# Block-sparse attention and a hard-swish MLP: values and their neighbour rows loaded by casting DMAs, head pairs p and p+4

## The chip, the cores and the metric

The kernel runs on one core of a Trainium2 chip. The metric is device time in microseconds (us); the profile's span goes from the first to the last instruction of one profiled execution.

## The reference

```python
B, H, S, D = 4, 8, 768, 64;  block, window = 32, 16;  scale = 1 / sqrt(D)
k_sum = max of k over each block of 32 rows       # 24 blocks a head
v_sum = mean of v over each block
scores_l = where(|i - j| < window, scale * q @ k.T, -1e9)
scores_s = scale * q @ k_sum.T + log(block)
a = softmax over [scores_l, scores_s]
x = a @ [v, v_sum]                                # (B, H, S, D) -> (B*S, H*D)
h = x @ w_in                                      # 512 -> 2048
out = (h * clip(h + 3, 0, 6) / 6) @ w_out         # 2048 -> 512
```

q, k, v, w_in, w_out and the output are f32. `kernel(q, k, v, moe_w_in, moe_w_out)` gives 3072 x 512.

## The kernel before, in words

**Tiles.** A query block is 64 rows, so a head has NQ = 12 of them. A query block sees at most 128 keys: its own 64 keys (partitions 0 to 63), the 24 block summaries (R_SUM = 64 to 87, with zeros to 95), the first 16 keys of the next block (R_NEXT = 96 to 111) and the last 16 of the block before (R_PREV = 112 to 127). `kx` holds these 128 key columns of each block, `qx` the transposed queries, `at` the exponentials, and `va[0]`, `va[1]` (even and odd batches) the 128 value rows in the same order, bf16. Two heads form a pair; a pair's rows in `va` are value of head j = 0, 64 columns between, value of j = 1, so that one 128 wide weight covers a head's values and the columns between, which hold zeros or (DEN_IN_VALUES, batches 2 and 3) the weights that give the softmax's denominator. Pairs are heads 2p and 2p+1.

**Attention of a batch b and pair p.** `Tk` (L484) transposes staged k on PE, copies it to `kx` on ACT (L502), reduces the block maxima on DVE (L513), spreads them over the blocks (L518), and copies the 16-column edges (L523, L525). `Tq` (L537) does the same for q (L550, L560). `Sc` (L573) makes the scores of half the query blocks (L591), their exp on ACT (L595), and the mask: batch 0 adds a mask on PE first (L586, `MASK_ON_PE`), the others multiply by 0 or 1 on DVE (L598). `AV` (L609) multiplies by the values (L625) and, in batches 0 and 1, by ones for the denominator (L630), takes 1/den as exp(-ln) on ACT (`lg`, L638 to L642), and writes `x` on DVE (L651 to L654). The value and denominator PSUM tiles have one buffer each.

**Feed-forward.** A tile t is half a batch, 384 rows of x. `F1(t, ft)` is four matmuls of 384 columns (`hp`, L678), a relu on ACT (`r`, L683) and a product on DVE (`g`, L686); `F2(t, j)` is three matmuls of 512 columns (L707); the copy out of PSUM is ACT's (L712), the store SP's (L714). F1 of a tile needs x of all four pairs.

**How v gets into `va` before.** Batches 0 and 1: `load_vf` (L252) reads v as f32 with 128 rows on the partitions; `cast_v` (L265) casts it into `va` on ACT, DVE and POOL; `edges_v` (L278, L279) copies the neighbours' rows from `va` to `va` with SP's DMAs, after the casts. Batch 0's block sums are matmuls with an indicator (`sum_v`, L736), copied by DVE (L740) and by POOL (`put_sums`, L751). Batches 2 and 3: `load_v` (L288) reads one head into `va` with a casting DMA, `edges_v` copies neighbours after all heads. Batches 1 to 3 get their block sums from `load_vrows` (L295), which reads 32 rows of a block into one partition, a tree of adds on POOL (`vsum`, L307) and SP's DMAs that write the sums into `va` (L311). `weights_between` and `zero_va1` (L757 to L774) fill the constant parts on POOL.

**What sets the order.** `Plan` (L33) collects every operation with an engine, a cost, a place in a list of slots, what it reads and writes and which buffers it takes; `order` (L63) simulates the engines with these costs and writes the instructions out in that order, each engine's in a fixed sequence. On the chip an engine waits at an instruction until its data are there, so nothing overtakes. All loads are issued by POOL, on one software queue, with eight completion semaphores in turn: a load's issue waits until the load eight before it has landed. The neighbour copies, sums and stores are issued by SP. The places are given by `first(p)` (L784) for batch 0, and by slots: F1 of tiles 0 and 1 in slots 0 to 31, F2 of tile 1 in 32 to 51, the loads of batch 1 at slot 14, its attention from slot 20, and so on (L809 to L874):

```python
    for b, s in ((2, 50), (3, 82)):
        at_slot(s, loads_kq, b, 0)
        at_slot(s + 8, loads_kq, b, 2)
        at_slot(s + 8.1, loads_v, b)
    for b in range(1, B):
        attention(b, 48 + 32 * (b - 1))
```

`first_loads_1` (L820) orders batch 1's loads, sums, casts and neighbour copies.

Of the kernel before, what the change touches and what calls it, by code (L numbers as in the profile page):

```python
# [25 lines left out]
NLONG = 4  # L26
NFILL = 100
MASK_ON_PE = (0,)
# [4 lines left out]
class Plan:  # L33
# [4 lines left out]
    BUFS = {"h": 2, "o": 2, "s": 2, "num": 1, "den": 1, "kq": 4, "g": 3, "x": 3, "vr": 2, "r": 3, "ot": 3, "lg": 2, "red": 2}  # L38
    CROSS = 0.18
    DMA_FIRST, DMA_SP = 1.4, 2.0  # L40
    WARM, SPARE = 7.0, 24.0
# [21 lines left out]
    def order(self):  # L63
# [3 lines left out]
        queue = 0.0  # L67
        given = {}

        turn = {q: [k for o in self.ops for pool, k in o["takes"] if pool == q] for q in ("x", "g", "vr")}  # L70
# [6 lines left out]
        while ready:  # L77
            cand = {}
            for i in ready:
# [7 lines left out]
                if any(pool in turn and turn[pool][len(given.get(pool, ()))] != key for pool, key in o["takes"]):  # L87
                    continue
                for n_th, (pool, key) in enumerate(o["takes"]):
                    old = given.get(pool, []) + [k for q, k in o["takes"][:n_th] if q == pool]  # L90
                    if len(old) >= self.BUFS[pool]:
                        for u in self.users.get(old[-self.BUFS[pool]], ()):
                            if end[u] is None:
                                ok = False
                                break
                            t = max(t, end[u] + self.CROSS)
                    if not ok:
                        break
                if ok:
                    cand.setdefault(o["eng"], []).append((t, o["place"], i))  # L100
# [17 lines left out]
            if o["dma"]:  # L118
                if o["eng"] == "POOL":
                    queue = max(queue, t + cost + self.DMA_FIRST) + o["dma"]  # L120
                    end[i] = queue
                else:
                    end[i] = t + cost + self.DMA_SP + o["dma"]
            for pool, key in o["takes"]:
                given.setdefault(pool, []).append(key)
# [24 lines left out]
def kernel(  # L150
# [43 lines left out]
    va = [const.tile([128, NP, NQ, 3, D], BF16, tag=f"va{i}", name=f"va{i}") for i in range(2)]  # L194
# [5 lines left out]
    def stage(which, b, p, half=None):  # L200

        if b == 0 and which == "k":
            return f"k{p // 2}", 2 * (p % 2), 4, RUN
        if b == 0:
            return f"q{half}", 2 * p, 8, RUN // 2
        return f"{which}{b}{p // 2}", 2 * (p % 2), 4, RUN
# [3 lines left out]
    def staged(which, b, p, half=None):  # L210
        name, i, n, r = stage(which, b, p, half)
        if name not in st_t:
            st_t[name] = ld.tile([128, 4 * RUN * D], BF16, tag="kq", name="stg", bufs=4)
        t = st_t[name]
        if b < NLONG:
            return t[0:RP].rearrange("p (h s d) -> p h s d", h=n, d=D), i
        return t[:, 0:2 * NT * 2 * D].rearrange("p (i s j d) -> p i s j d", i=2, j=2, d=D), i // 2

    def load(which, b, p, n, half=None):
        src = (k if which == "k" else q)[b, 2 * p:2 * p + 2 * n]  # L220
        name, i, heads, r = stage(which, b, p, half)

        def issue():
            t, i = staged(which, b, p, half)
            lo, hi = (0, S) if half is None else (half * HALF, (half + 1) * HALF)
            nc.gpsimd.dma_start(out=t[:, i:i + 2 * n, 0:r], in_=src[:, lo:hi].rearrange("h (p s) d -> p h s d", s=r))

        def issue_rows(u, j):
            t, i = staged(which, b, p)
            nc.gpsimd.dma_start(out=t[:, i + u, :, j], in_=src[2 * u + j].rearrange("(s p) d -> p s d", p=128))  # L230

        keys = [f"{which}{b}{p + u}{half}" for u in range(n)]
        takes = () if name in taken else (("kq", name),)
        taken.add(name)
        if b < NLONG:
            plan.add("POOL", 0.72, place(), issue, (), keys, takes, dma=(1.2 if r == RUN else 0.73) * n)
            plan.uses(name)
        else:
            for u in range(n):
                for j in range(2):  # L240
                    plan.add("POOL", 0.82, place(), lambda u=u, j=j: issue_rows(u, j), (), [keys[u] + str(j)], takes, dma=1.5)
                    plan.uses(name)
                    takes = ()

    def load_vf(b, p, n):

        def issue():
            if b not in vf_t:
                vf_t[b] = gp.tile([128, H, NT, D], F32, tag="g", name="vf")
            t = vf_t[b][:, 2 * p:2 * p + 2 * n].rearrange("r h s d -> r (h s) d")  # L250
            src = v[b, 2 * p:2 * p + 2 * n].rearrange("h s d -> (h s) d")
            nc.gpsimd.dma_start(out=t, in_=src.rearrange("(s r) d -> r s d", r=128))  # L252

        name = f"vf{b}"
        plan.add("POOL", 1.05 if n == 1 else 1.2, place(), issue, (), [f"{name}{p + u}" for u in range(n)],
                 () if name in taken else (("g", name),), dma=1.65 * n)
        plan.uses(name)
        taken.add(name)

    def cast_v(eng, b, p, odd, lo, hi):  # L260

        def op():
            t = vf_t[b][64 * odd:64 * odd + 64, 2 * p:2 * p + 2, lo:hi]
            copy = eng.copy if eng is nc.scalar else eng.tensor_copy
            copy(va[b % 2][0:QB, p, 2 * lo + odd:2 * hi:2, 0:3:2].rearrange("r t j d -> r j t d"), t)  # L265

        n = hi - lo
        e, cost = {nc.scalar: ("ACT", 0.1 + 0.11 * n), nc.vector: ("DVE", 0.07 + 0.08 * n),
                 nc.gpsimd: ("POOL", 0.1 + 0.13 * n)}[eng]
        plan.add(e, cost, place(), op, [f"vf{b}{p}"], [f"va{b % 2}{p}o{2 * s + odd}" for s in range(lo, hi)])  # L270
        plan.uses(f"vf{b}")

    def edges_v(b, p0, p1, lo, hi):

        def op():
            o = va[b % 2][:, p0:p1].rearrange("r p t j d -> r p t (j d)")
            a, z = max(lo, 1), min(hi, NQ - 1)
            nc.sync.dma_start(out=o[R_PREV:, :, a:hi], in_=o[QB - EDGE:QB, :, a - 1:hi - 1])  # L278
            nc.sync.dma_start(out=o[R_NEXT:R_PREV, :, lo:z], in_=o[0:EDGE, :, lo + 1:z + 1])  # L279

        ps = range(p0, p1)
        plan.add("SP", 1.1, place(), op,
                 [f"va{b % 2}{p}{o}{t}" for p in ps for t in range(max(lo - 1, 0), min(hi + 1, NQ)) for o in "oP"],
                 [f"va{b % 2}{p}e{t}" for p in ps for t in range(lo, hi)], dma=0.35 * (p1 - p0))

    def load_v(b, h):
        def issue():
            nc.gpsimd.dma_start(out=va[b % 2][0:QB, h // 2, :, 2 * (h % 2)], in_=v[b, h].rearrange("(t r) d -> r t d", r=QB))  # L288

        plan.add("POOL", 0.8, place(), issue, (), [f"va{b % 2}{h // 2}{'oP'[h % 2]}{t}" for t in range(NQ)], dma=1.5)  # L290

    def load_vrows(b, g):
# [5 lines left out]
        plan.add("POOL", 0.6, place(), issue, (), [f"vr{b}{g}"], (("vr", f"vr{b}{g}"),), dma=3.2)  # L298

    def vsum(b, g):  # L300
# [8 lines left out]
        def put(i):  # L309
            h = 4 * g + i  # L310
            nc.sync.dma_start(out=va[b % 2][R_SUM:R_SUM + NB, h // 2, :, 2 * (h % 2)],  # L311
# [3 lines left out]
        while n > 1:  # L315
            n //= 2
            plan.add("POOL", 0.15 + 0.14 * n, place(), lambda n=n: add(n), (), [f"vr{b}{g}"])
        for i in range(4):
            p = (4 * g + i) // 2
            plan.add("SP", 0.6, place(), lambda i=i: put(i), [f"vr{b}{g}"], [f"va{b % 2}{p}{'sS'[i % 2]}{half}" for half in range(2)], dma=0.4)  # L320

    vs_t, taken, where = {}, set(), [-1000.0]
# [8 lines left out]
    w_in_v = moe_w_in.rearrange("(kt p) f -> p kt f", p=128)  # L331
    w_out_v = moe_w_out.rearrange("(ft p) m -> p ft m", p=128)

    def load_w_in(c):
        def issue():
            w = d_ff // 4
            nc.gpsimd.dma_start(out=w_in_sb[:, :, c * w:(c + 1) * w], in_=w_in_v[:, :, c * w:(c + 1) * w])

        plan.add("POOL", 0.78, place(), issue, (), [f"wi{c}"], dma=3.3)

    def load_w_out(c):
# [4 lines left out]
        plan.add("POOL", 0.78, place(), issue, (), [f"wo{c}"], dma=3.3)  # L346
# [6 lines left out]
    zero = const.tile([128, 1], F32, tag="zero", name="zero")  # L353
# [16 lines left out]

    at_place(-999)
    load("k", 0, 0, 1)
# [7 lines left out]
    load("q", 0, 0, 2, 0)  # L380
    load_vf(0, 0, 1)
    load("k", 0, 1, 1)
# [22 lines left out]
    load_vf(0, 1, 1)  # L405
    load("k", 0, 2, 2)
    load("q", 0, 2, 2, 0)
    at_place(-998)
    op("POOL", 2.6, c_mask, ["band"], ["maskb"])
    load_vf(0, 2, 1)  # L410
    load_vf(0, 3, 1)
    load_w_in(0)
    load_w_in(1)
    at_place(-262)
    load("q", 0, 0, 4, 1)
    load_w_in(2)
    at_place(-242)
    load_w_in(3)
# [10 lines left out]
    def fill():  # L429
        t = ps_n.tile([128, 512], F32, tag="den", name="fill")  # L430
        nc.tensor.matmul(t[:], idle[:, 0:128], idle[:], start=True, stop=True)
# [9 lines left out]
    def c_kx():  # L441
        nc.vector.memset(zero[:], 0.0)
# [4 lines left out]
    op("DVE", 0.5, c_kx, (), ["zero"] + both("kxc", NP))  # L447

    def c_va0():
# [5 lines left out]
        nc.vector.memset(va[0][R_NEXT:, :, 0:NQ:NQ - 1].rearrange("r p t j d -> r p t (j d)").bitcast(F32), 0.0)  # L455
# [453 lines left out]
```

## Time and profile before

| | |
|---|---|
| three runs | 269.53, 268.74, 267.88 us; median 268.74 |
| profiled execution | 267.68 us, of it span 266.0 us; mean granted TensorE clock 0.972 |
| busy | PE 236.4 us (89%), DVE 159.1 (60%), ACT 165.6 (62%), POOL 115.2 (43%) |
| DMA | software queue 19.93 MB in 25,504 packets; hardware queue 9.34 MB in 11,648 |
| loads on POOL's queue, median issue to landing | k 7.4, q 7.6, vr 13.7, one head of v 7.2, w_in 11.3, w_out 17.9 us |

Slices are fortieths of the span (6.65 us); their digits are tenths busy. Matmuls are pipelined, so their busy time overlaps and is more than their share of the path: a group of four F1 matmuls follows the one before it after 0.65 us, though each is recorded as 0.33. An idle engine that nothing waits for costs nothing.

### The profile page before, as it was taken

Reading aid. Unit: us, or ns where it says so; the run is one execution under the profiler, and the core shown is the slowest. Engines: PE = TensorE matmul, PEld = TensorE weight load, DVE = VectorE, ACT = ScalarE, POOL = GpSimd, SP = SyncE. Lnnn points to the kernel's source line nnn. Section 1 sums busy time; section 2 is a strip of 40 time slices with the busy share of each in tenths; the row PEclk is TensorE's granted clock in tenths of the full one; section 3 lists DMA queues with packets and bytes.
Section 4 is the critical chain, followed back from the end, with each engine's and each line's share of the span. In section 5 each row is a group of like instructions: output and inputs, shape, how many; then the busy total and the mean of one; then the engine's idle time right before and its main releaser. Section 6 shows DMA issues by size and latency. Waiting matters only on the chain.

```text
span 266.0 us, 5782 instructions
## 1 busy us (share of the span) xinstructions
PE 236.4 (89%) x2286; PEld 128.3 (48%) x2286; DVE 159.1 (60%) x300; ACT 165.6 (62%) x323; POOL 115.2 (43%) x160
## 2 busy tenths in 40 slices
PE   7997679999862599599989999999999899999994
PEld 1564345555430255356545555555555555555541
DVE  3575456477894033978988558787864654444410
ACT  5375568665440247569878777878994864654520
POOL 8979759984996016997899200000000000000000
PEclk9999999999997599979999999999999999999998
DMA  5999999999918999916996271101011011111112
GB/s 92 202 229 211 217 195 235 208 213 208 99 30 148 244 239 146 126 22 123 221 162 88 66 123 39 42 0 43 24 57 39 2 41 39 42 39 41 39 42 79
DMA packets 37180, 29.65 MB, mean 111 GB/s; under 512 B 21088, under 2 KB 32224, under 8 KB 36576
## 3 DMA queue, kind: packets, MB, share of 16 engines
q0 software_dynamic: 25504, 19.93, 47.4%
q1 hardware_dynamic: 11648, 9.34, 13.5%
q8 instruction: 18, 0.29, 0.5%
q14 instruction: 10, 0.08, 0.1%
HBM read 31.98 MB, written 6.29 MB: 144 GB/s over the span
## 4 chain that ended last, share of the span: by engine, by line
PE 61%; DMA 14%; POOL 9%; ACT 5%; DVE 5%; issue 3%; SPq 2%; POOLq 0%; ACTq 0%
PE op L707 24%; PE hp L678 23%; DMA stg<-in_q_dram 8%; DMA va<-va 5%; POOL vr L307 4%; PE nd L625 3%; PE sp L591 2%; PE sums L736 2%; PE tpk L494 2%; PE tpq L550 2%; POOL va L751 2%; PE nd L630 1%; ACT r L683 1%; SPq L311 1%; POOL va L265 1%
## 5 line engine op out<-in xcount | busy, mean ns | idle before, releaser
L678 PE MATMUL hp<-x,win 128*128 128x384 bf16 x512 | 96.9, 330 | 6.8 <-DVE g L686 5.1
L683 ACT ACTIVATE r<-hp,half_c 128x384 f32<-128x384 f32 x128 | 72.2, 579 | 45.7 <-PE hp L678 41.1
L707 PE MATMUL op<-wout,g 128*128 128x512 bf16 x384 | 95.6, 384 | 0.3 <-DVE g L686 0.3
L686 DVE SCALAR_TENSOR_TENSOR g<-r,hp 128x384 bf16<-128x384 f32 x128 | 68.0, 550 | 38.0 <-ACT r L683 35.2
L678 PEld LDWEIGHTS <-win 128*128 128x128 bf16 x512 | 48.3, 98 | 41.9 <-issue 8.4
L707 PEld LDWEIGHTS <-g 128*128 128x128 bf16 x384 | 35.7, 99 | 37.3 <-issue 2.0
L307 POOL TENSOR_TENSOR vr<-vr 96x1024 f32<-96x1024 f32 (+3 forms) x24 | 30.9, 1286 | 1.5
L595 ACT ACTIVATE at<-sp 128x384 bf16<-128x384 f32 x64 | 27.7, 487 | 4.5 <-PE sp L591 4.4
L625 PE MATMUL nd<-at,va 128*128 128x64 bf16 x384 | 16.9, 195 | 13.1 <-DMA va<-va 11.1
L625 PEld LDWEIGHTS <-va 128*128 128x128 bf16 x384 | 14.9, 99 | 18.8 <-issue 12.6
L654 DVE TENSOR_TENSOR x<-nd,lg 128x384 bf16<-128x384 f32 x16 | 8.9, 557 | 22.8 <-ACT lg L642 22.7
L598 DVE TENSOR_TENSOR at<-at,mask 128x768 bf16<-128x768 bf16 x24 | 18.5, 771 | 6.7 <-ACT at L595 6.5
L641 ACT ACTIVATE lg<-nd 128x384 f32<-128x384 f32 x16 | 7.9, 492 | 20.3 <-PE nd L630 20.1
L757 POOL MEMSET va<- 32x768 bf16 (+1 forms) x24 | 17.6, 735 | 6.0 <-PE nd L625 5.2
L712 ACT COPY ot<-op 128x512 f32<-128x512 f32 x24 | 14.0, 585 | 9.2 <-PE op L707 8.8
L513 DVE TENSOR_REDUCE red<-tpk 128x24 bf16<-128x768 bf16 x16 | 15.3, 954 | 6.7 <-ACT kx L502 6.5
L502 ACT COPY kx<-tpk 128x768 bf16<-128x768 bf16 x16 | 12.8, 798 | 8.3 <-PE tpk L494 8.2
L523 POOL COPY kx<-kx 128x176 bf16<-128x176 bf16 x8 | 2.7, 333 | 34.2 <-ACT kx L502 32.7
L642 ACT ACTIVATE lg<-lg 128x384 f32<-128x384 f32 x32 | 16.7, 523 | 1.0
L651 DVE TENSOR_TENSOR x<-nd,lg 64x384 bf16<-64x384 f32 x16 | 8.8, 547 | 12.6 <-ACT lg L642 11.6
L560 DVE COPY qx<-tpq 128x768 bf16<-128x768 bf16 (+1 forms) x16 | 13.6, 849 | 3.5 <-PE tpq L550 3.5
L288 POOL DMA_DIRECT2D va<-in_v_dram x16 | 12.0, 765 | 5.0 <-DMA vf<-in_v_dram 4.5
(63 smaller groups left out, 197.7 us busy)
## 6 DMA issues: line engine op xcount, KB each, us to landing
out_dram<-ot SPq DMA_DIRECT2D x24, 256.0 KB
vr<-in_v_dram POOLq DMA_DIRECT2D x6, 768.0 KB, 13.7
stg<-in_k_dram POOLq DMA_DIRECT2D x7, 384.0 KB, 7.4
stg<-in_q_dram POOLq DMA_DIRECT2D x7, 384.0 KB, 7.6
win<-in_moe_w_in_dram POOLq DMA_DIRECT2D x4, 512.0 KB, 11.3
wout<-in_moe_w_out_dram POOLq DMA_DIRECT2D x4, 512.0 KB, 17.9
vf<-in_v_dram POOLq DMA_DIRECT2D x4, 384.0 KB, 6.7
vf<-in_v_dram POOLq DMA_DIRECT2D x2, 768.0 KB, 18.7
```

The costliest lines, as they stand in the source:

```text
L307: nc.gpsimd.tensor_tensor(out=o, in0=r[:, 0:n], in1=r[:, n:2 * n], op=ALU.add)
L513: nc.vector.tensor_reduce(red[0][:], tp[:].rearrange("p (s n c) -> p n s c", s=RUN, n=NB), axis=AX.XY, op=ALU.max)
L595: nc.scalar.activation(a[:, j], sp_t[keys[j]][:], AF.Exp, scale=scl)
L598: nc.vector.tensor_tensor(a, a, msk.unsqueeze(1).to_broadcast([128, 2, NH, QB]), op=ALU.mult)
L625: nc.tensor.matmul((num, den)[j * two][:, u * QB:(u + 1) * QB], w[:, j * D:j * D + 128], a[:, j, t], start=two or (u == 0 and j == 0), sto ...
L642: nc.scalar.activation(lg[:], lg[:], AF.Exp, scale=-1.0)
L678: nc.tensor.matmul(hp[:], w_in_sb[:, kt, ft * 128:(ft + 1) * 128], xt[t][:, kt], start=(kt == 0), stop=(kt == NP - 1))
L683: nc.scalar.activation(r[:], c[0][:], AF.Relu, bias=half_c[:], scale=1.0 / 6.0)
L686: nc.vector.scalar_tensor_tensor(gt[t][:, ft], c[1][:], 1.0, c[0][:], op0=ALU.min, op1=ALU.mult)
L707: nc.tensor.matmul(ops[t, ts][:], gt[t][:, ft, ts * 128:(ts + 1) * 128], w_out_sb[:, ft], start=(ft == 0), stop=(ft == NFT - 1))
L712: nc.scalar.copy(o[:], ops[t, ts][:])
L757: nc.gpsimd.memset(va[i][r0:r1, p, :, 1], float(w))
```

## The change

- Pairs are heads p and p+4. `va` becomes [128, 48, 3, 64], with 48 = pair x block, so that one DMA can write a side j of all pairs; w_in's rows are read in the matching order, in two DMAs of 64 partitions each, a quarter of the columns first and then the rest.
- `cast_v` stays for batch 0 alone. Batch 1 loads v as batches 2 and 3 do, and all three in two DMAs of four heads.
- `edges_v` reads the neighbours' rows from memory with casting DMAs on POOL's queue, four a batch, batch 0 too; they no longer depend on `va`'s other rows.
- k and q of batches 1 to 3 come in two DMAs of four heads into stages of eight heads (3 buffers for 4 of half the size); batch 0's come by pairs.
- Sums of batches 1 to 3 come from row reads as before; batch 0's are put by DVE (first half) and POOL.
- No mask on PE; batch 0 multiplies on DVE as the others do.
- The constant columns are filled by one or two larger memsets; the filling matmuls use 32 weight columns.
- The planner's costs for DMAs change, and it knows the limit of eight.

```diff
-MASK_ON_PE = (0,)
+MASK_ON_PE = ()
-    BUFS = {... "kq": 4, ...}
+    BUFS = {... "kq": 3, ...}
-    DMA_FIRST, DMA_SP = 1.4, 2.0
-    WARM, SPARE = 7.0, 24.0
+    DMA_FIRST, DMA_LAND, DMA_SP, DMA_LIMIT = 0.7, 0.45, 2.5, 8
+    WARM, SPARE = 10.0, 24.0
...
+                if o["dma"] and o["eng"] == "POOL" and len(landed) >= self.DMA_LIMIT:
+                    t = max(t, landed[-self.DMA_LIMIT])
...
-    va = [const.tile([128, NP, NQ, 3, D], BF16, tag=f"va{i}", name=f"va{i}") for i in range(2)]
+    NV = NP * NQ
+    va = [const.tile([128, NV, 3, D], BF16, tag=f"va{i}", name=f"va{i}") for i in range(2)]
+    vj = [t[:, :, 0:3:2].rearrange("r n j d -> r j n d") for t in va]
...
-    def edges_v(b, p0, p1, lo, hi):
-        def op():
-            o = va[b % 2][:, p0:p1].rearrange("r p t j d -> r p t (j d)")
-            a, z = max(lo, 1), min(hi, NQ - 1)
-            nc.sync.dma_start(out=o[R_PREV:, :, a:hi], in_=o[QB - EDGE:QB, :, a - 1:hi - 1])
-            nc.sync.dma_start(out=o[R_NEXT:R_PREV, :, lo:z], in_=o[0:EDGE, :, lo + 1:z + 1])
+    def edges_v(b):
+        def issue(j, r0, first, rows, at):
+            src = v[b, NP * j:NP * j + NP].rearrange("h (t r) d -> r (h t) d", r=QB)
+            nc.gpsimd.dma_start(out=vj[b % 2][r0:r0 + EDGE, j, first:first + NV - 1], in_=src[rows, at:at + NV - 1])
+        for j in range(2):
+            for r0, first, rows, at in ((R_NEXT, 0, slice(0, EDGE), 1), (R_PREV, 1, slice(QB - EDGE, QB), 0)):
+                plan.add("POOL", 0.8, ...)
-    def load_v(b, h):
+    def load_v(b, j):
         def issue():
-            nc.gpsimd.dma_start(out=va[b % 2][0:QB, h // 2, :, 2 * (h % 2)], in_=v[b, h].rearrange("(t r) d -> r t d", r=QB))
+            nc.gpsimd.dma_start(out=vj[b % 2][0:QB, j],
+                                in_=v[b, NP * j:NP * j + NP].rearrange("h (t r) d -> r (h t) d", r=QB))
...
-    w_in_v = moe_w_in.rearrange("(kt p) f -> p kt f", p=128)
+    w_in_v = moe_w_in.rearrange("(j p d) f -> j d p f", j=2, d=D)
+    W_IN = ((0, 1), (1, 4))
     def load_w_in(i):
+        lo, hi = (c * (d_ff // 4) for c in W_IN[i])
+            nc.gpsimd.dma_start(out=w_in_sb[64 * j:64 * j + 64, :, lo:hi], in_=w_in_v[j, :, :, lo:hi])   # j = 0, 1
...
-    load("k", 0, 0, 1); ident; load("q", 0, 0, 2, 0); load_vf(0, 0, 1); load("k", 0, 1, 1); load_vf(0, 1, 1)
-    load("k", 0, 2, 2); load("q", 0, 2, 2, 0); c_mask; load_vf(0, 2, 1); load_vf(0, 3, 1)
-    load_w_in(0); load_w_in(1); load("q", 0, 0, 4, 1); load_w_in(2); load_w_in(3); load_w_out(0..3)
+    load_pair("k", 0); ident; load_pair("q", 0, 0); load_pair("k", 1); load_pair("q", 1, 0); load_vf(0); load_vf(2)
+    load_pair("k", 2); c_mask; load_pair("q", 2, 0); load_pair("k", 3); load_pair("q", 3, 0); load_vf(1); load_vf(3)
+    edges_v(0); load_w_in(0); load("q", 0, slice(0, H), "1", 1); load_w_in(1); load_w_out(0..3)
...
-        nc.tensor.matmul(t[:], idle[:, 0:128], idle[:], start=True, stop=True)
+        nc.tensor.matmul(t[0:32], idle[:, 0:32], idle[:], start=True, stop=True)
...
+    def c_between(eng, i, weights):
+        if not weights:
+            eng.memset(words(va[i][:, :, 1]), 0.0)
+        else:
+            for rows, w in ((slice(0, 128), 1.0), (slice(R_SUM, R_NEXT), float(BLK))):
+                eng.memset(words(va[i][rows, :, 1]), two_of(w))
...
-    def first_loads_1(): k, q of pairs 0, 1; vrows; k, q of pairs 2, 3; zero_va1; vf; vsum; casts; edges
-    def loads_v(b): vrows; weights_between; load_v x8; vsum; edges_v
+    def loads_kq(b):
+        for which in "kq":
+            load(which, b, slice(0, NP), "A")
+            load(which, b, slice(NP, H), "B")
+    def loads_v(b):
+        if b < 3 or 1 not in DEN_IN_VALUES:
+            between(nc.gpsimd, b % 2, b in DEN_IN_VALUES)
+        load_vrows(b, 0); load_vrows(b, 1); load_v(b, 0); load_v(b, 1); edges_v(b); vsum(b, 0); vsum(b, 1)
-    for b, s in ((2, 50), (3, 82)):
-        at_slot(s, loads_kq, b, 0)
-        at_slot(s + 8, loads_kq, b, 2)
-        at_slot(s + 8.1, loads_v, b)
+    for b, s in ((1, 12), (2, 50), (3, 82)):
+        at_slot(s, loads_kq, b)
+        at_slot(s + 0.1, loads_v, b)
```

Several of these lines are drawn together from longer ones (`...`, and calls of the loads in a row); the instructions are those of the change.

## The prediction

> **What bounds the kernel now.** I read the page's slices first, then the waits, then the windows, then the chain of work that ended last.
>
> ```profile
> PE   7997679999862599599989999999999899999994
> DVE  3575456477894033978988558787864654444410
> POOL 8979759984996016997899200000000000000000
> PEclk9999999999997599979999999999999999999998
> DMA  5999999999918999916996271101011011111112
> ```
>
> A slice is 6.65 us. From slice 21 on PE is nearly full; its holes lie in the first five slices and at slices 11 to 13, where DVE and POOL empty as well and the granted clock falls right behind. While that hole opens the DMA engines are not the limit (slice 11 has 1).
>
> ```profile
> PE nd L625 <- DMA va<-va: 11.1, 3, 8.0
> DVE at L598 <- ACT at L595: 6.5, 11, 2.3
> PE hp L678 <- DVE g L686: 5.1, 7, 2.4
> ```
>
> Columns: total us, times, longest. One wait of 8.0 us is for the copies of neighbouring v rows (va<-va), the longest wait of PE.
>
> ```profile
> 0.00:30.40 30.40, 23.90 (x273) 13.41 (x274) 15.73 (x52) 16.78 (x31) 26.56 (x46) 1.00 1.06 187
> 30.40:49.20 18.80, 17.12 (x206) 10.13 (x206) 11.15 (x22) 14.37 (x30) 13.81 (x18) 1.00 1.24 216
> 49.20:81.20 32.00, 28.44 (x261) 14.57 (x259) 24.76 (x41) 16.54 (x30) 26.06 (x31) 1.00 0.97 149
> 81.20:89.30 8.10, 0.07 (x3) 0.08 (x3) 1.45 (x4) 0.00 (x0) 2.95 (x5) 0.65 0.98 169
> 89.30:110.30 21.00, 19.13 (x252) 10.35 (x253) 9.34 (x16) 12.28 (x25) 8.87 (x15) 0.89 1.04 191
> 110.30:262.30 152.00, 147.79 (x1297) 79.72 (x1296) 96.71 (x168) 105.05 (x207) 36.90 (x49) 0.99 0.30 62
> ```
>
> Windows by stage: length, then busy time of PE, PEld, DVE, ACT, POOL, then granted clock, DMA share and GB/s. Stage 1 ends where the first feed-forward group has all of x; 2 is F1 of tile 0; 3 is F1 of tile 1 and F2 of tile 0; 4 is the hole; 5 is F2 of tile 1 with batch 1's attention; 6 ends with the last matmul. A tail of 3.7 us follows, and 1.7 us lie outside the span: 30.4 + 18.8 + 32.0 + 8.05 + 21.05 + 152.0 + 3.7 + 1.7 = 267.7, the profiled execution's own 267.68. The three runs' median of 268.74 lies 1.06 above it; a change of about 1% is what a measurement of this kernel can tell from none.
>
> What released the hole, from the chain in order of time (start, us, what):
>
> ```profile
> 46.52 18.30 DMA stg<-in_q_dram
> 65.11 0.75 POOL va L288
> 65.92 2.36 POOL vr L307
> ...
> 77.71 0.77 POOL va L265
> ...
> 81.72 0.61 SPq L278
> 82.38 6.74 DMA va<-va
> 89.25 0.80 PE nd L625 x12
> ```
>
> POOL issues batch 2's v loads until 65.9 (each DMA on it waits until the one eight before has landed), only then folds batch 1's block sums (two trees, to 77.7), then casts; SP puts the sums and issues the neighbour copies behind them, and those take 6.74 us to land. So it is POOL's order and SP's queue, not bandwidth.
>
> **The change, part by part.**
>
> *Batch 1's v (stage 4).* Removed: 8 casts on POOL and DVE (DVE's 4 at 1.18 us), 8 neighbour copies on SP. Added: 2 loads of 3,072 rows and 4 neighbour loads of 752 rows, each row 128 B in SBUF, on POOL's queue. The nearest row is batch 2's load of one head (768 such rows): eight landings from 65.47 to 70.82, 0.76 us apart, and 0.63 apart at 140.4 to 142.3. I take 0.68: 2.7 us a load, 0.65 a neighbour DMA. The two f32 loads replaced took 6.9 (landings 56.48 to 63.42); the new six take 8.0. Bounds of a neighbour DMA, which fills only 16 partitions: 0.4 (its bytes at the row loads' 229 GB/s) and 6.7, the landing of a present neighbour copy; I stay near 0.65, since rows and packets are those of the load.
>
> The Trainium skill ("DMA: Bandwidth & Descriptors", Specifications) wants at least 512 B per transfer for full rate and says that smaller ones are read, modified and written, which speaks against this part. The row agrees in kind (96 KB in 0.68 us are 145 GB/s against 229), and 0.68 already holds it; taking the page as double the 0.4 us at full rate, an estimate from that page, a neighbour DMA would cost 0.8 and the sum would grow by 0.6 us in stage 1.
>
> When is batch 1 ready? Weights landed at 42.89; the prologue's four neighbour DMAs add 2.6, some of the SP copies' interference (0.33 share at 30 to 35) goes, so about 44. Then k and q four at 2.1 (52.4), two row reads at 3.5 (59.4), v 5.4 (64.8), neighbours 2.6 (67.4). In the changed program's order POOL issues the row reads and v ahead of batch 2, then two memsets, four neighbour issues, one k load that waits for the first row read (55.9), then the trees: 56.6 to 68. Queued behind them are batch 2's loads, which wait for nothing near. SP puts the first four sums, then an output store that waits for F2 of tile 0's last block (about 72), then the other four: pair 0 complete at 74.7. PE gets there at 78.5 (below), 3.8 us of cover. Stage 4 becomes 0 (0 to 4).
>
> *Prologue (stage 1).* Neighbours: the ten SP issues and their 1.4 and 1.7 us waits go; all four pairs now wait for four neighbour DMAs. Queue: k in pairs 4.8, then q, k, q, vf, vf to 11.2, k 12.5, (mask work on POOL holds the next issue) q 13.4, k, q 15.2, vf, vf 18.8, neighbours 21.4, first quarter of w_in 23.9, second q half 26.4, rest of w_in 33.9. DVE decides: after vf at 18.8 it still does, in its order, 4 casts at 0.48, 2 mask products at 0.56, 2 sums at 0.29 and their copies at 0.45, a reduce at 0.96, spread and edges 0.9, 2 q copies and 4 x at 0.56: 9.7 us, and about 1.3 of waits for the lg of the last two pairs; last x at 29.8. The sum copy on DVE has no row of its own: between 0.23 (288 elements broadcast, L518) and 0.82 (the same copy on POOL); taken 0.45, four of them span -0.9 to +1.5. The larger memsets (1,536 elements, double a 0.70 row) sit in DVE's idle start. Filling matmuls on 32 columns are as long as before (512 columns stream); a later warm clock would cost up to 3 us (sums 2.77 cold, 1.43 warm). Stage 1: 29.8 (28 to 34).
>
> *Mask off PE (b0).* 8 pairs of matmuls at 0.42 (32.26 to the score at 32.68) go, 3.4 us, half of it in stage 1 under waits. Eight products come at 0.56 (free DVE; the mean of 0.77 mixes in collisions). Stage 2 is then ACT's: 16 r at 0.58, 8 exp at 0.44, 4 lg at 1.0 are 16.8, plus 0.7 to the first r: 17.5 (17 to 19.5; the rest of w_in at 33.9 meets its first user, after four F1, two scores and a value, at 34.0: no cover).
>
> *Stage 3.* PE's work is 16 F1 and 20 F2 at 0.65, 8 transposes at 0.46, 2 scores at 0.29: 27.7. Before it was 27.2 and 4.8 was lost, mostly to DVE casts and products under POOL's trees (2.42 of it before 77.89). Casts go; the trees move into this stage's middle and still hit products:
>
> ```profile
> L598 DVE TENSOR_TENSOR at<-at,mask 128x768 bf16<-128x768 bf16 x24 | 18.5, 771 | 6.7 <-ACT at L595 6.5
> L265 DVE CAST va<-vf 64x768 bf16<-64x768 f32 x4 | 4.6, 1180 | 0.1
> ```
>
> The 16 free products mean 0.56, the 8 under a tree 1.19. I take 3.5 lost: 31.2 (29 to 33). The Trainium skill ("SBUF — State Buffer", Who interferes with whom) says that DVE and GpSimd lock each other out of a shared port pair, descriptor writing included: new POOL DMAs would stall under DVE copies. Here a k or q issue took 0.65 to 0.79 us everywhere, so the sum stays; by the page, an issue that meets one DVE copy waits for its end; with the copies' 0.5 us for each of the 12 issues ahead of the trees the cover of 3.8 above would be gone and stage 4 would grow by 2.
>
> *Stage 5.* Work: 12 F2 7.8, 5 values 3.4, 5 scores 1.5, 3 transposes 1.4: 14.1. The clock hole (half speed 83.66 to 93.90) cost 2.0 and goes. One num and den buffer makes five values a chain of 5 x (0.68 + 1.02 + 0.56 + waits), 13 at least; batch 2's first tree now falls here. I take 18.5 (16 to 21).
>
> *Stage 6.* One value and a q transpose move in (1.1), a score moves out (0.3), tree collisions of 1.75 at 111 partly go: 152.0 (149 to 154). Batch 2's second tree starts after tpk of pair 1, ends 10 us later, its puts 3 us ahead of use. K and q in fours, w_in in halves, 2 memsets of 1.4 for 12 of 0.74: hidden by POOL's slack from 150 on; without it 2 to 3 us.
>
> Sum: 29.8 + 17.5 + 31.2 + 0 + 18.5 + 152.0 + 3.7 + 1.7 = 254.4, or 13.3 under 267.68; by the median 255.4. I give 254.5.
>
> **The rivals.**
> - PE full (0.18): losses halve in stages 1, 3, 5 and 6. For: 4 of 5 holes have a named releaser that goes. 28.5 + 17 + 29.5 + 16.5 + 150 + 5.4 = 246.9.
> - Late prologue (0.17): sum copies at 0.82, a cold clock, w_in late: +6, 260.5. For: DVE's chain has no slack.
> - Sums late (0.08): POOL's trees or SP's queue, with 3.8 of cover, slip by 8: hole of 4, colder clock 2: 260.
> - Neighbour DMAs are slow (slower, 0.08): at the 6.7 us of the present copies, four ahead of w_in cost 24 instead of 2.6: +21.4, 276. The gain is used up from 0.65 + 13.3/4 = 4.0 us each. Against: those copies move 4,224 B rows under other traffic.
> - Nothing moves (0.04): the hole reappears before batch 2's values, 267.
>
> **How the numbers follow.** Forecast, 251 to 258: 0.45. Faster takes all but the last two rivals: 0.88, same 0.04, slower 0.08. The range 246 to 264 reaches over the faster rivals.
>
> **What would show it.** PE without a gap over 3 us between 60 and 95; one clock-0.5 record fewer; neighbour landings 0.6 to 0.8 us apart; trees starting before 60; first F1 at 29 to 31; batch 2's values waiting for no DMA. A neighbour landing above 2 us, a tree after 62, or a gap at the first w_in user above 2 us would prove a step wrong.

## The result, and the profile after

The changed kernel took 253.14 us (median of four executions, 252.78 to 255.89) beside 269.13 us for the kernel before on the same chip: ratio 0.9435, 95% interval 0.936 to 0.9509. The forecast was 254.5. The profiled execution took 252.96 us, of it span 251.3. Ratios leave disturbed executions out; for one kernel below (`cast_b1`) too few remained for a ratio, and it is given as four bare times.

The slices of the changed kernel (6.28 us each now; the rows of PEld, the weight loads, and of ACT are left out):

```profile
PE   5899699999993997999989999999999999999993
DVE  5568888658871237999687798468674735444400
POOL 8985962757997704769990010000000000000000
PEclk9999999999997799999999999999999999999999
DMA  5999999999989999419992101100111021011112
```

The hole at slices 11 to 13 has shrunk to one slice (12), and the low clock from three slices to two; of PE's smaller holes in the first eleven slices, only the one in slice 4 is still there. What is left is named by PE's longest waits (total us, times, longest):

```profile
PE nd L618 <- DMA va<-vs: 3.7, 1, 3.7
PE fill L429 <- DVE band L390: 1.8, 1, 1.8
```

The 8.0 us for va<-va, the neighbour copies, are gone. In their place stands one wait of 3.7 us for va<-vs: the sums that SP puts. The windows of the same stages (length, busy time of PE, PEld, DVE, ACT, POOL, granted clock, DMA share, GB/s):

```profile
0.00:32.50 32.50, 25.21 (x298) 14.90 (x299) 21.87 (x64) 15.31 (x29) 26.71 (x48) 1.00 1.19 174
32.50:47.50 15.00, 14.83 (x170) 8.99 (x170) 11.93 (x25) 13.75 (x30) 6.78 (x9) 1.00 1.23 205
47.50:75.93 28.43, 27.95 (x273) 14.96 (x277) 20.67 (x38) 16.58 (x30) 23.29 (x25) 1.00 1.51 199
75.93:79.96 4.03, 0.34 (x8) 0.24 (x6) 0.46 (x3) 0.00 (x0) 3.48 (x5) 0.83 1.72 189
79.96:98.38 18.42, 16.62 (x206) 8.74 (x209) 6.50 (x12) 11.72 (x25) 6.45 (x10) 0.85 1.57 200
98.38:247.30 148.92, 145.87 (x1303) 79.99 (x1318) 96.32 (x172) 105.59 (x208) 31.08 (x41) 1.00 0.32 62
```

| stage | before | forecast | after |
|---|---|---|---|
| 1 prologue, until x of tile 0 | 30.4 | 29.8 | 32.5 |
| 2 F1 of tile 0 | 18.8 | 17.5 | 15.0 |
| 3 F1 of tile 1, F2 of tile 0 | 32.0 | 31.2 | 28.4 |
| 4 hole ahead of batch 1's values | 8.05 | 0 | 4.0 |
| 5 F2 of tile 1, batch 1 | 21.05 | 18.5 | 18.4 |
| 6 the rest | 152.0 | 152.0 | 148.9 |
| tail and outside the span | 5.4 | 5.4 | 5.7 |
| sum | 267.7 | 254.4 | 253.0 |

Stages 2 and 3 are now PE at work nearly without a gap (14.83 of 15.00 and 27.95 of 28.43). The chain that ended last shows where the hole of stage 4 comes from (start, us, what):

```profile
68.96 1.96 PE op L700 x9
...
70.94 0.59 ACT ot L705
...
71.55 0.34 SPq L707
...
72.00 7.82 DMA va<-vs
79.82 0.14 issue
79.96 0.48 PE nd L618 x6
```

POOL had batch 1's last sum at 69.67. SP's queue first had the store of F2 of tile 0's last block, which waited for PE and ACT, then the first of four puts that write the second heads' sums, that of pair 0, 36 KB, issued at 72.00 and landed 7.82 us later.

### The profile page after: what moved, and what is told of

Same layout as the page of the kernel before. It is cut to its first block, busy times and chain, and to the rows that moved or that the text cites. A ratio compares the mean times of both kernels' runs of the same rounds, so it can differ in the third digit from the quotient of the medians.

```text
span 251.3 us, 5636 instructions
## 1 busy us (share of the span) xinstructions
PE 230.8 (92%) x2247; PEld 127.8 (51%) x2273; DVE 157.8 (63%) x309; ACT 163.5 (65%) x321; POOL 97.8 (39%) x134
## 4 chain that ended last, share of the span: by engine, by line
PE 79%; ACT 6%; DVE 5%; DMA 5%; issue 2%; POOL 1%; SPq 0%; ACTq 0%; POOLq 0%
PE hp L672 31%; PE op L700 30%; PE nd L618 4%; DMA va<-vs 3%; PE sums L729 3%; PE sp L584 3%; PE tpq L549 2%; PE fill L429 2%; PE tpk L504 2%; DMA stg<-in_k_dram 2%; PE nd L623 2%; DVE at L591 1%; ACT at L588 1%; ACT lg L635 1%; DVE g L680 1%
## 5 line engine op out<-in xcount | busy, mean ns | idle before, releaser
L677 ACT ACTIVATE r<-hp,half_c 128x384 f32<-128x384 f32 x128 | 71.9, 580 | 35.7 <-PE hp L672 32.1
L672 PE MATMUL hp<-x,win 128*128 128x384 bf16 x512 | 94.3, 326 | 0.7 <-DVE g L680 0.5
L700 PE MATMUL op<-wout,g 128*128 128x512 bf16 x358 | 90.0, 385 | 2.6 <-issue 1.8
L588 ACT ACTIVATE at<-sp 128x384 bf16<-128x384 f32 x64 | 27.7, 486 | 6.0 <-PE sp L584 5.9
L295 POOL TENSOR_TENSOR vr<-vr 96x1024 f32<-96x1024 f32 (+3 forms) x24 | 30.0, 1252 | 1.4
L591 DVE TENSOR_TENSOR at<-at,mask 128x768 bf16<-128x768 bf16 x32 | 21.9, 683 | 9.0 <-ACT at L588 8.8
L618 PE MATMUL nd<-at,va 128*128 128x64 bf16 x384 | 17.1, 194 | 6.7 <-DMA va<-vs 3.7
L705 ACT COPY ot<-op 128x512 f32<-128x512 f32 x24 | 14.1, 587 | 12.8 <-PE op L700 12.8
L618 PEld LDWEIGHTS <-va 128*128 128x128 bf16 x384 | 15.2, 98 | 11.9 <-issue 7.8
L647 DVE TENSOR_TENSOR x<-nd,lg 128x384 bf16<-128x384 f32 x16 | 8.9, 556 | 14.1 <-ACT lg L635 14.0
L584 PEld LDWEIGHTS <-kx 64*128 64x128 bf16 x384 | 7.6, 96 | 12.4 <-issue 11.4
L266 POOL DMA_DIRECT2D va<-in_v_dram x16 | 11.4, 715 | 4.2 <-DMA va<-in_v_dram 2.1
```

Of the source, the lines that this page charges most:

```text
L295: nc.gpsimd.tensor_tensor(out=o, in0=r[:, 0:n], in1=r[:, n:2 * n], op=ALU.add)
L584: nc.tensor.matmul(sp[j][:, u], kx[rows, p, t], qx[rows, p, t * QB:(t + 1) * QB], start=not on_pe, stop=not on_pe or u == NH - 1)
L588: nc.scalar.activation(a[:, j], sp_t[keys[j]][:], AF.Exp, scale=scl)
L591: nc.vector.tensor_tensor(a, a, msk.unsqueeze(1).to_broadcast([128, 2, NH, QB]), op=ALU.mult)
L618: nc.tensor.matmul((num, den)[j * two][:, u * QB:(u + 1) * QB], w, a[:, j, t], start=two or (u == 0 and j == 0), stop=two or (u == NH - 1 ...
L672: nc.tensor.matmul(hp[:], w_in_sb[:, kt, ft * 128:(ft + 1) * 128], xt[t][:, kt], start=(kt == 0), stop=(kt == NP - 1))
```

## The experiments

### The order of the work, and the path of the data

The change does two things at once: it gives the planner the limit of eight loads and other costs, and it brings v by other DMAs. `no_limit` is the changed kernel with the old planner, `limit_alone` the kernel before with the new one.

```diff
 no_limit, in the changed kernel:
-    DMA_FIRST, DMA_LAND, DMA_SP, DMA_LIMIT = 0.7, 0.45, 2.5, 8
-    WARM, SPARE = 10.0, 24.0
+    DMA_FIRST, DMA_LAND, DMA_SP, DMA_LIMIT = 1.4, 0.0, 2.0, 10 ** 6
+    WARM, SPARE = 7.0, 24.0
 limit_alone, in the kernel before:
-    DMA_FIRST, DMA_SP = 1.4, 2.0
-    WARM, SPARE = 7.0, 24.0
+    DMA_FIRST, DMA_LAND, DMA_SP, DMA_LIMIT = 0.7, 0.45, 2.5, 8
+    WARM, SPARE = 10.0, 24.0
+                if o["dma"] and o["eng"] == "POOL" and len(landed) >= self.DMA_LIMIT:
+                    t = max(t, landed[-self.DMA_LIMIT])
...
```

> The changed kernel with the planner's DMA constants of before and without its limit of eight (the data path stays). POOL's order then has batch 2's k, the memsets, batch 2's v and neighbour loads ahead of batch 1's trees; their issues wait for landings of batch 1 (69.4 for the last). Theory A (the order of the trees on POOL is what closed the hole): trees 70 to 81 in place of 58.7 to 69.7, second put of pair 0 lands at 83 to 84, PE waits about 8 us from 76 and works some 4 us at half clock after it: 258 us (256 to 261). Theory B (loading v and its neighbours without casts and copies is what closed it, wherever the trees stand): within 1.5 us of 253.

> The kernel before with the planner's new DMA constants and its limit of eight alone (casts, SP copies, pairs as before). The trees move ahead of 5 of batch 2's 8 head loads. Theory A: trees from about 59 in place of 65.9, casts done at 75 in place of 81, copies landed at 83 in place of 89: 5 us less, 263 (261 to 265). Theory B: the casts and the 6.7 us of the copies keep the hole, 267 to 269.

`no_limit`: 262.37 us, ratio 0.9744 (0.9663 to 0.9825). PE's two longest waits, and the chain that ended last:

```profile
PE nd L618 <- DMA va<-vs: 6.1, 1, 6.1
PE nd L618 <- POOL vr L295: 4.1, 1, 4.1
```

```profile
65.01 1.35 POOL va L275
66.37 2.76 POOL va L266 x4
...
69.19 2.38 POOL vr L295
...
79.87 0.33 POOL vs L295
...
80.21 5.64 DMA va<-vs
...
85.99 0.48 PE nd L618 x6
```

POOL issues batch 2's loads first and starts the trees at 69.19, 10.5 us later than in the changed kernel (58.65). PE waits 4.1 us for the trees and 6.1 for the put behind them. That is theory A, with a loss a little above the 256 to 261 it allowed.

`limit_alone`: 258.93 us, ratio 0.9636 (0.9559 to 0.9713), lower than the 261 that A allowed. With the old casts and copies, and the trees at 57.61 instead of 65.92, PE's hole before batch 1's values fell from 8.0 to 3.4 us, and it is the copy that lands late, 6.37 us after its issue:

```profile
PE nd L628 <- DMA va<-va: 6.7, 3, 3.4
...
75.79 0.79 SPq L314
...
77.34 6.37 DMA va<-va
83.72 0.14 issue
83.85 0.80 PE nd L628 x12
```

So by the medians 10.2 of the 16.0 us come without any change to the data's path, and 6.8 come without the order (269.13 less 262.37; the interval of `no_limit` says 1.8 to 3.4%). The two add up to 17.0, a little more than the 16.0 of both together, and the difference is within the intervals.

### Why a put of 36 KB takes 7.8 us

While the first put was under way, from 72 to 76, SP issued all four puts of the second half, and the trace's DMA view of that window lists the packets that moved:

```profile
DMA packets 437, 1.04 MB, mean 260 GB/s; under 512 B 16, under 2 KB 352, under 8 KB 352
...
q0 software_dynamic: 437, 1.04, 113.0%
...
va<-vs SPq DMA_DIRECT2D x4, 36.0 KB
```

All 437 are of the software queue, POOL's loads: 1,024 B packets of k, then 8,192 B ones of batch 2's row read, which POOL issued at 69.6 and 70.3 as soon as its trees were done. The hardware queue, SP's, moved nothing in these 4 us; its store ran from 76, its puts from 77. Theory C, put on record before the runs: without those loads beside them the puts land in time. Two kernels take the loads away in different manners.

```diff
 put_pool:
-            nc.sync.dma_start(out=vj[b % 2][R_SUM:R_SUM + NB, g, NQ * i:NQ * i + NQ],
+            (nc.gpsimd if b == 1 else nc.sync).dma_start(out=vj[b % 2][R_SUM:R_SUM + NB, g, NQ * i:NQ * i + NQ],
...
 pause:
+        if b == 1:
+            for n in range(4):
+                op("POOL", 1.4, lambda: nc.gpsimd.memset(pause[:], 0.0), ["vr11"], ["pause"])
```

> The changed kernel with batch 1's eight sum puts issued by POOL into the loads' queue right after each tree, ahead of batch 2's loads, instead of by SP. Theory C (the put that PE waited 3.7 us for was issued at 72.0 but stood behind the k and row-read packets of the loads' queue until 77): puts land by 74, no wait of PE for values of batch 1, no half clock at 78.6 to 85.4: 248.5 (247.5 to 250). Theory D (a put of 288 small packets takes its 7.8 us anywhere): the wait stays, 252 to 254.

> The changed kernel with four more POOL memsets of 1.4 us (scratch) between batch 1's trees and batch 2's loads, so that no load's packets run while SP's puts land. Theory C: the put issued at about 72 lands within 3 us, the wait and the half clock go, batch 2's loads come 5.5 us later and are still early enough: 249 (248 to 251). Theory D: the put takes 7.8 us as before: 253 or more.

`put_pool`: 249.70 us, ratio 0.9261 (0.9196 to 0.9325), clear of the changed kernel's interval. `pause`, which adds 5.6 us of useless work on POOL: 249.60 us, 0.9255 (0.9183 to 0.9327). Batch 1's first value in each, by the chain that ended last (`put_pool`, then `pause`), follows F2 and the scores with no wait; against the 75.93 at which PE was ready in the changed kernel, the planner's new order brings PE there 2.7 us later in `put_pool` and 0.5 later in `pause`:

```profile
75.67 2.70 PE op L700 x12
78.37 0.28 PE sp L584 x12
78.65 0.46 PE nd L618 x12
```

```profile
74.49 2.05 PE op L701 x9
76.54 0.35 PE nd L619 x12
76.89 0.33 PE nd L624 x2
```

The trace's completion events of the second four puts (issue, then last completion, us):

```
after     72.00 79.82   72.86 80.27   73.69 80.95   74.51 81.67    SP, loads from 69.6
pause     72.44 74.66   73.31 76.77   74.14 76.95   74.96 82.19    SP, loads from 74.84
put_pool  72.72 75.69   73.38 76.56   74.19 78.99   74.83 79.15    POOL's queue, ahead of the loads
```

`pause` holds its own control: three puts ahead of the first k load took 2.2 to 3.5 us, and the fourth, issued 0.12 us after that load, took 7.2. In `put_pool` the clock stays full (no low digit after the start):

```profile
PEclk9999999999999999999999999999999999999999
```

Theory C stands. The hole of 4 us gone brought 3.4; the half clock behind it (6.83 us in the changed kernel, none in `put_pool`) therefore seems to have cost little of its own, in a stage where five values in a row wait for ACT and DVE as well; since `put_pool` has another order too, that is not shown.

That the packets of the loads hold up a put, and not POOL's work of issuing them, is seen later in the changed kernel's own trace. POOL issues no DMA between 120.6 and 131.6, while loads issued before that still land until 131.6: four puts issued from 126.5 to 129.2 took 5.3, 4.6, 3.9 and 3.3 us, beside packets of 128 B, and the next one, issued at 132.3 with nothing beside it, took 2.2.

### The prologue

Stage 1 missed its forecast by 2.7 us. Two causes were put on record: the narrower fills leave the clock low for longer, or the neighbour loads hold up the last f32 rows of v.

```diff
 fill128:
-        nc.tensor.matmul(t[0:32], idle[:, 0:32], idle[:], start=True, stop=True)
+        nc.tensor.matmul(t[:], idle[:, 0:128], idle[:], start=True, stop=True)
 edges0_sp:
-    edges_v(0)
...
         cast_v(nc.vector, p, 1, 0, 3)
+        copy_edges0(p, 0)        # SP copies from va[0], as before, a pair and half each
...
```

> The changed kernel with the filling matmuls on 128 columns again, as before; nothing else differs. Theory G: the fills of 32 columns leave the granted clock low until 17.1 us (before: 12.0), the first sums of v run cold (24 matmuls 4.7 us where a later group takes 2.8), and that is a part of the 2.7 us by which stage 1 missed the forecast: full clock by 12.5, last x at 30 to 31 instead of 32.0, time 251.5 (250.5 to 252.3). Theory H: stage 1 is set by the last f32 rows of v, which land at 21.8, and by DVE's chain behind them: full clock early, last x within 0.7 of 32.0, time 253 (252.3 to 254).

> The changed kernel with batch 0's neighbour rows copied by SP out of the cast rows, a pair and half at a time, as before; the four neighbour loads of the prologue go. Theory N: the neighbour loads' 128 B packets share the queue with the last f32 rows of v and hold them up: the rows land at 19.5 or earlier instead of 21.8, the first quarter of w_in at 24.5 instead of 27.1, last x at 30 to 31, time 251.5 (250.5 to 252.3). Theory S: the copies wait for the casts and land 1.4 us or more behind them, so what is won on the queue is lost on PE: last x at 32 to 34, time 254 (252.5 to 256).

`fill128`: 252.78 us, 0.9418 (0.938 to 0.9456), as H has it: the last x ends at 32.1, in the changed kernel at 32.55 (the 32.0 on record is its start). G falls by its own test: the first full-clock record stands at 16.9 us with fills of either width (17.1 in the changed kernel), and the first 24 sums take 4.73 us in both. What made the clock rise at 12.0 in the kernel before stays open; the width of the fills is not it.

`edges0_sp`: 258.27 us, 0.9628 (0.9572 to 0.9684), slower than either theory had it. The last rows of v land at 20.45 instead of 21.83, so the neighbour loads delay them by 1.4 us; but PE's waits up to 40 us show what comes for it:

```profile
PE nd L629 <- DMA va<-va: 6.0, 3, 3.0
```

Three waits of up to 3.0 us for the copies, and the last x at 38.6. The granted clock fell as well, to half from 21.0 to 24.4 and from 31.3 to 41.5, so the loss is that of the waits and of the clock together. The four neighbour loads of batch 0 are thus worth 5 us to the changed kernel, in its order.

Two kernels, built on `put_pool`, move loads in the prologue, and one puts the mask back on PE.

```diff
 vf_early:
     load_pair("q", 2, 0)
+    load_vf(1)
+    load_vf(3)
     load_pair("k", 3)
     load_pair("q", 3, 0)
-    load_vf(1)
-    load_vf(3)
 win_early:
-    load("q", 0, slice(0, H), "1", 1)
     load_w_in(1)
+    load("q", 0, slice(0, H), "1", 1)
 mask_pe (in the changed kernel):
-MASK_ON_PE = ()
+MASK_ON_PE = (0,)
```

> The kernel with batch 1's puts on POOL's queue (249.7 us, last x at 31.75), and in the prologue the last two f32 loads of v issued ahead of k and q of pair 3. Theory V (stage 1 is the landing of the last f32 rows of v and 10 to 11 us of DVE behind it): they land at 19.5 to 20.5 instead of 21.4, last x at 30 to 31; PE then meets the rest of w_in at 36.6, so little of it is seen in the time: 249.2 (248.4 to 250). Rival K (the chain from pair 3's k through its reduce, score and value has no slack either): k lands at 20.5 to 22, last x at 32 to 34, time 250.8 (250 to 252.5).

> The kernel with batch 1's puts on POOL's queue (249.7 us), and the rest of w_in issued ahead of the second halves of batch 0's q. Theory W (w_in's rest at 36.6 is what PE waits for, 0.8 us, at its first user): it lands at 34 to 35, the wait goes, time 249.0 (248.3 to 249.6). Rival Q (the second halves of q, at 36 to 37 instead of 29.6, come late for ACT and DVE, whose work for the second half of batch 0 already fills stage 2): PE waits 1 to 4 us before 52, time 251.5 (250 to 254).

> The changed kernel with the mask of batch 0 added by PE again (eight pairs of matmuls of 0.42 us) instead of multiplied in by DVE (eight products of 0.56 us). Theory P, the prediction's step: PE pays 3.4 us, half of it under waits in stage 1: 254.8 (254 to 256), with the loss in stage 2. Theory Q: DVE is what decides stage 1, so that stage 1 gets shorter by about what stage 2 gets longer: 253 (252.2 to 253.8).

`vf_early`: 248.73 us, 0.9262 (0.9216 to 0.9307); the lowest median of all, though its interval doesn't separate it from `put_pool`. The rows of v land at 18.64 (in `put_pool` at 21.97), earlier than V asked, and the last x comes at 31.9, just as in `put_pool` (31.75). The time lies in V's range and not in K's, but V is wrong as the whole story. Pair 3's k now lands at 20.6 (in `put_pool` at 14.7), and DVE reduces it from 24.1 in its order, without a wait of its own for it; from 26 on DVE waits for ACT's `lg`. That the two chains are equally long is likely, since the four loads that feed them, k and q of pair 3 and the two of v, end at 20.9 and 22.0 in the two orders, but not shown.

`win_early`: 250.06 us, 0.9286 (0.9248 to 0.9324), no different from `put_pool`. In its profiled execution (254.90 us, 4.8 above the median, so it decides little) the rest of w_in landed at 35.35 instead of 36.62 and the last x came at 32.6 instead of 31.75. The interval, 248.7 to 250.8 us, holds W's 249.0 and no gain at all, and only the lower end of Q: not settled, and too small to matter.

`mask_pe`: 254.61 us, 0.9467 (0.9419 to 0.9516). The interval overlaps the changed kernel's. The windows have the loss where theory P puts it: last x at 32.5 as without, and tile 1's first F1 at 51.05 instead of 49.44, 1.6 us later.

### Batch 1's values the old way, in the new order

`cast_b1` gives batch 1 its f32 loads, casts and SP copies back; `copy_edges` only the copies, for batches 1 to 3; `cast_put` is `cast_b1` with the puts of `put_pool`.

```diff
 cast_b1, loads_v, in effect for batch 1:
-        for j in range(2):
-            load_v(b, j)
-        edges_v(b)
+            load_vf1(0)
+            load_vf1(1)
...
+            for p in range(NP):
+                cast_v1(nc.gpsimd, p, 0)
+                cast_v1(nc.vector, p, 1)
+            for p in range(NP):
+                copy_edges(p)
```

> The changed kernel with batch 1's v loaded as f32, cast by POOL and DVE, and its neighbours copied by SP, as before; the planner and everything else as in the change. Theory A (the gain is the order: the trees moved ahead of batch 2's loads): PE waits 3 to 5 us for batch 1's values, as in the changed kernel, time 254.5 (253 to 257). Theory B (the gain is batch 1's new path): the copies of neighbours come behind casts and puts and take 6 us to land again, PE waits 7 to 9 us, time 259 (257.5 to 262).

> The changed kernel with the neighbours of batches 1 to 3 copied by SP out of the v rows, as before; v itself still comes by casting DMAs, and batch 0 is as in the change. Theory E (the neighbours read from memory are worth several us): the copies wait behind the puts and stand still behind the loads of batch 2 as the puts do, and PE waits 5 to 8 us for batch 1, time 257 (255 to 261). Rival F (the copies end with the puts, which PE waits for anyway): wait 3 to 4.5 us, time 253.5 (252 to 254.5).

> The kernel with batch 1's puts on POOL's queue (249.7 us), and batch 1's v loaded as f32, cast by POOL and DVE, its neighbours copied by SP, as before. Theory B (batch 1's new path is worth several us in itself): the neighbour copies behind the casts land 5 to 7 us after their issue and PE waits 3 to 8 us for them, or DVE's casts under POOL's trees cost as much: 255.5 (253.5 to 259). Theory A (with the trees early and the puts out of SP's queue the old path fits under PE's other work too): 250.5 (249 to 252).

`cast_b1`: 261.81, 261.20, 260.55 and 255.37 us: three in B's range and the fastest in A's, so it doesn't decide; and without the wait that B named, for PE has no long wait for va<-va. `copy_edges`: 254.84 us, 0.9488 (0.943 to 0.9546), only just beyond F: the neighbours of batches 1 to 3 read from memory are worth 1.7 us by the medians, within both intervals. The wait that E and F both named isn't there either: in its profiled execution (257.03 us) PE waits for no DMA before batch 1's values, which the planner's new order places at 89.8 instead of 75.9, and the granted clock is half from 95.6 to 109.3.

`cast_put` decides what `cast_b1` left unclear: 262.71 us, 0.9716 (0.9669 to 0.9764), 13 us behind `put_pool` and beyond B's 259. B's first reason is wrong again. Of its second the casts hold and the trees don't: batch 1's trees end at 74.8, and DVE's casts run from 74.5 to 80.0 beside POOL's own. A part of the chain that ended last, the group of casts, and the windows from 76 on:

```profile
73.64 0.87 DVE qx L583
74.54 5.49 DVE va L263 x4
80.07 0.56 DVE at L619
...
98.11 0.75 PE nd L646 x12
```

```profile
L263 DVE CAST va<-vf 64x768 bf16<-64x768 f32 x4 | 5.5, 1432 | 0.0
```

```profile
76.00:97.00 21.00, 14.14 (x181) 7.50 (x183) 13.54 (x19) 8.09 (x16) 13.54 (x19) 0.99 1.00 193
97.00:117.00 20.00, 16.64 (x200) 10.72 (x196) 13.56 (x20) 10.44 (x20) 12.61 (x20) 0.50 1.12 175
```

The four casts run at 1.43 us each and keep DVE from F1's products and batch 1's masks for 5.5 us; PE's longest wait for DVE's g is 2.6. The planner, told of casts, puts and copies in a row, places the first values at 98.1, where `put_pool` has them at 78.65. PE works 14.1 of the 21 us between (`put_pool`: 20.0 of 22.0 from 76 to 98), and after that runs 20 us at half clock. So it is not a late DMA that PE waits for: with the old path the plan pushes a whole stage back.

That is the price of this plan, and not of the old path as such. Each of these edits makes the planner write a new order for all engines, so path and order are not taken apart: `limit_alone`, with the whole data path of the kernel before, SP's copies and puts included, takes 258.93 us, 3.8 less than `cast_put`; and the first values come late in `copy_edges` (89.8) too, at a cost of 1.7 us.

## Why the prediction was right, and where it was off

- **The order released the hole, as said.** "It is POOL's order and SP's queue, not bandwidth": the order alone is worth 10.2 us (`limit_alone`), and what was left of the hole, there and in the changed kernel, is the late landing of a DMA of SP's.
- **Stage 4, the mis-sized term.** The step "pair 0 complete at 74.7" took it that a put lands 2 us or so after its issue; it took 7.8, since it stood still behind POOL's loads. The trees ended at 69.67 (forecast 68) and the store left at 71.55 (forecast "about 72"), so this landing is nearly all of the error. The bound of stage 4, "0 to 4", held it. PE also came earlier than forecast, at 75.9 instead of 78.5. The rival "sums late" named the place and the size of the hole; it missed the total because other stages gained more.
- **The total is closer than its parts, and that is in part luck.** Stages 1 and 4 and the tail came 2.7, 4.0 and 0.3 us above the forecast, stages 2, 3, 5 and 6 2.5, 2.8, 0.1 and 3.1 below; the sum is off by 1.4. Two of the signs failed: PE has a gap of more than 3 us (3.7), and the first F1 came at 32.4, not at 29 to 31. The rival "PE full" was nearer in stages 2, 3 and 6, but had no hole and 28.5 for stage 1. In the rival of slow neighbour DMAs a sum slipped: four at 6.7 us are 26.8, not 24, which gives 279 for 276.
- **Stage 1.** The queue step failed: the last rows of v landed at 21.83, not 18.8, 3.0 late, 1.4 of it by the neighbour loads' packets (`edges0_sp`). Pair 3's q still landed in time, at 15.36 for 15.2; the two loads of v behind it took 6.5 us for 3.6, and 5.1 in `edges0_sp`, so they were taken too short by 1.5 of their own. DVE's work behind was 10.7 us against a sum of 11.0. The sum copy, taken at 0.45 with no row of its own, measured 0.44. What the removal of SP's copies is worth was priced by the "1.4 and 1.7 us waits" of the kernel before; in the new order the copies would cost 5 us (`edges0_sp`).
- **Stage 2.** The step "stage 2 is then ACT's, 16.8" added recorded durations. Between 32.5 and 47.5 ACT's 30 instructions add up to 16.2 us by count and mean, but to 13.75 of busy time: its recorded durations overlap. PE set the stage. The rest of w_in landed at 36.74 instead of 33.9 and met its first user at 36.88: the slip of stage 1 covered the slip of the queue, and the two stages together took 47.5 against a forecast of 47.3.
- **Stage 3.** The work on PE was right (27.7 forecast, 27.95 busy), the 3.5 us of loss wasn't: 0.5. Before, PE waited 3.6 us for DVE's `g` in this stage, now not at all. DVE's idle time is much the same (7.2 us of 32.0 before, 7.8 of 28.4 now), so it is likely the casts that made the difference: with them back, PE's wait for `g` is 5.1 us in all (`cast_put`).
- **Stage 5** came at 18.4 for 18.5, though with a half clock that wasn't forecast, so this is luck in part; **stage 6** at 148.9 for 152.0, 0.1 below its lower bound, and no run here takes apart why.
- **Neighbour DMAs** landed 0.36 to 0.91 us apart in the prologue and 0.62 to 1.41 in batch 1, 0.73 in the mean over both, for 0.65 taken. The estimate of 0.8 from the Trainium skill ("DMA: Bandwidth & Descriptors", Specifications) is as close. The lock that "SBUF — State Buffer" (Who interferes with whom) warns of is not seen in POOL's issues: those of k, q, neighbours and weights took 0.61 to 0.82 us throughout (1.35 to 1.38 for 3,072 rows).

## What to carry to other kernels

When a profile shows a wait for a small DMA, look at what its queue and the other queue move in that window before you price it: here a 36 KB put took 2.2 to 3.5 us alone and 7.2 to 7.8 beside loads, and issuing it in the loads' own queue, ahead of them, brought it to 3.0 to 4.8 and cured the wait. A planner that knows the real limits of its queue was worth more here than the new data path (10.2 us alone against 6.8), so test the two apart. Copies that wait for casts can cost by their landing (`edges0_sp`) or by where the plan puts the work behind them (`cast_put`): look at which it is.

## What the runs showed of the hardware

SP's hardware queue moved no packet for 4 us while POOL's software queue had 437 packets under way, and later in the same trace the two ran beside each other, from 77 on, when the software queue's packets were 128 B. The Trainium skill ("DMA: Bandwidth & Descriptors", Queues, rings and completion order) says that each DMA engine takes turns between the queues that have work, a packet at a time, and that such a packet holds typically 9 to 17 descriptors and at most 64. Whether what the trace counts as a packet is one of these or a single descriptor, no run here tells, so 437 to none neither bears the page out nor refutes it. In `pause`, the fourth put's packets started again at 79.5 beside k's 1,024 B packets, so size alone does not explain it. What does stays open: a kernel with one put beside loads of one packet size each would tell, and was not tried.
